# Attention into a gated MLP: 8 block transfers a pair in place of 16, two T buffers, two shared slots for the probabilities, four separate convolution products

## The chip, the cores and the metric

One core of a Trainium2 chip runs the whole program in one launch. The metric is the time of one execution in microseconds. Five queues of instructions run beside each other and wait for one another by semaphores: TensorE (PE, with its weight loads as PEld), VectorE (DVE), ScalarE (ACT), GpSimd (POOL) and SyncE (SP), which here issues nearly all transfers. The sixteen DMA engines that carry out the transfers belong to no queue of instructions.

## The reference

Decay attention over 8 batches of 8 heads, 576 positions, 64 wide, and behind it a gated MLP with a causal convolution of 5 taps:

```python
scores = (q @ k.T) / 8 ; decay = cum[:, None] - cum[None, :]      # cum = cumsum(log(clip(f)))
scores = where(causal, -1e9, scores + decay)
attn = exp(scores - max) ; attn = attn / (sum(attn) + 1e-9)
x = (attn @ v) laid out as (batch, seq, 512)
gate = sigmoid(sum_k conv_w[k] * x[t - 4 + k])                    # 5 taps, per channel
out = (gate * (x @ w_val)) @ w_out
```

## The kernel before, in words

The work is cut into 32 pairs, i = 0 to 31: two heads of one batch. Four pairs make a batch, and the MLP of a batch (`plan_moe`) follows when its four pairs are done.

A pair goes through these steps. `load_pair` brings q and k (`Xr`, two buffers), `load_rest` v (`vt`). `plan_t` splits `Xr` into a rounded part `Xh` (a copy, L286) and a rest `Xl` (a subtraction, L399). `plan_s` makes the scores in four groups u = 0 to 3: the key tile of 576 columns (tile 3), of 448 (tile 2), of 320 and 192 together (tiles 1 and 0), and the last 64 rows. PE writes scores to PSUM; DVE adds the mask and takes the row minimum of the negated scores (L478); ACT takes the exponential into SBUF (L482), for tiles 3 to 0 into `Pt`, which has a place of its own for each tile and head, one set for all pairs, and for the last rows into `Pl`. The sums become reciprocals on DVE (L491, L492), which go by way of DRAM (`zd`) into `zb`, spread over the partitions.

`plan_pt` turns the probabilities. DVE transposes 32 x 32 blocks of each tile from `Pt` into `Tt` (L515, four instructions a pair of 1152, 896, 640 and 384 elements for both heads) and of `Pl` (L518). What is turned inside a block has still to move to other partitions: that is a transfer from `Tt` to `U` (two buffers) for each of 4 groups of 32 partitions and 2 halves of the columns, and each in two pieces m, one with tile 3 (576 columns) and one with the rest (992): 16 transfers of 32 partitions each, issued on SP by the helper `load` (L298). There is one `Tt`, so the transposes of pair i + 1 wait until the transfers of pair i that read the same piece have landed. `plan_pv` multiplies `U` with `vt`, scales by `zb` into `x32` (L563, L286), splits that into `xh` and `xl` (L286, L575), and makes the gate: for pairs 0 to 3 by matmuls with diagonal weights `dg`, for the other 28 by five taps, the first a product (L291 or L293), the next `NA - 1` each a product into `tm` (L291 or L293) and an addition (L606), the rest a fused multiply-add on DVE (L608). Then tanh (L610). `plan_moe` makes value (`Mv`) and output (`Mo`) matmuls, with H (L636), `hh` (L286), `hl` (L650) and the output copy (L677) between.

The two weight matrices are loaded in four pieces each and decoded from 64-bit words (`plan_w`, `decode`), by turns in the memory of `ot` and in `wu`.

What runs when is not left to a scheduler at run time. Every step is a node with the engines it may run on and an estimated duration; the order of all nodes, the engine of each and the PSUM bank of each result are read from the constant `ORDER`, a compressed list of numbers (node times 8 plus an engine code). So each queue runs its steps strictly in the order of the list, and a step that has to wait holds everything behind it on its queue.

## Time and profile before

| | us |
|---|---|
| time, median of 3 runs | 645.98 (645.62 to 647.64) |
| profiled execution, its own time | 645.04 |
| profiled execution, span from the first to the last instruction | 643.3 |

The page gives for each engine its busy time in the span. A busy share is an average over stages: the start (weights, masks, first pairs) and the end (the last MLP) look different from the long middle, in which pair follows pair. A wait is put down to what came last, and an idle stretch of an engine that nobody waits for costs nothing.

### The profile page before, as it was taken

Reading aid. Unit: us, or ns where it says so; the run is one execution under the profiler, and the core shown is the slowest. Engines: PE = TensorE matmul, PEld = TensorE weight load, DVE = VectorE, ACT = ScalarE, POOL = GpSimd, SP = SyncE. Lnnn points to the kernel's source line nnn. Section 1 sums busy time; section 2 is a strip of 40 time slices with the busy share of each in tenths; the row PEclk is TensorE's granted clock in tenths of the full one; section 3 lists DMA queues with packets and bytes.
Section 4 is the critical chain, followed back from the end, with each engine's and each line's share of the span. In section 5 each row is a group of like instructions: output and inputs, shape, how many; then the busy total and the mean of one; then the engine's idle time right before and its main releaser. Section 6 shows DMA issues by size and latency. Waiting matters only on the chain.

```text
span 643.3 us, 16239 instructions
## 1 busy us (share of the span) xinstructions
PE 519.6 (81%) x6096; PEld 451.4 (70%) x6096; DVE 460.6 (72%) x1163; ACT 326.0 (51%) x912; POOL 248.9 (39%) x283
## 2 busy tenths in 40 slices
...
GB/s 236 102 233 196 213 199 165 196 137 121 128 207 223 189 170 178 154 190 165 185 186 207 193 204 188 187 179 197 227 167 210 213 171 191 232 146 154 143 34 82
DMA packets 62558, 114.12 MB, mean 177 GB/s; under 512 B 15760, under 2 KB 32144, under 8 KB 62480
## 3 DMA queue, kind: packets, MB, share of 16 engines
...
q14 instruction: 30, 0.25, 0.1%
...
## 4 chain that ended last, share of the span: by engine, by line
DMA 28%; PE 25%; SPq 20%; DVE 15%; ACT 5%; issue 4%; POOL 1%; DVEq 0%; ACTq 0%; POOLq 0%
PE banks L271 25%; SPq L298 20%; DMA Xr<-in_x_dram 13%; DMA U<-T 7%; DVE banks L478 4%; DVE T L515 4%; DMA zb<-zd 2%; ACT P L482 2%; DMA zd<-zt 2%; DMA vt<-in_v_dram 2%; DVE gate L608 2%; ACT Xh L286 1%; DMA ot<-in_w_val_dram 1%; DVE x L563 1%; DMA gate<-in_f_dram 1%
## 5 line engine op out<-in xcount | busy, mean ns | idle before, releaser
L482 ACT ACTIVATE P<-banks,negm 128x192 f32<-128x192 f32 (+3 forms) x256 | 145.8, 580 | 51.4 <-DVE negm L478 50.6
L515 DVE STREAM_TRANSPOSE T<-P 128x896 f32<-128x896 f32 (+3 forms) x128 | 119.1, 956 | 53.7 <-DMA U<-T 44.7
L478 DVE CUSTOM_DVE_ANT_0 banks<-banks,mk 128x320 f32<-128x320 f32 (+3 forms) x256 | 137.4, 581 | 26.6 <-PE banks L271 17.1
L271 PE MATMUL banks<-U,vt 64*64 64x128 f32 (+1 forms) x3456 | 120.3, 284 | 36.4 <-DMA U<-T 25.9
L271 PEld LDWEIGHTS banks<-U,vt 64*64 64x64 f32 x3456 | 115.0, 152 | 47.3 <-issue 20.7
L271 PE MATMUL banks<-xh,wall 128*128 128x288 f32 x512 | 122.1, 323 | 26.1 <-ACT P L482 16.6
L271 PEld LDWEIGHTS banks<-xh,wall 128*128 128x128 f32 x512 | 93.2, 208 | 32.1 <-ACT P L482 18.9
L271 PE MATMUL banks<-wall,hh 128*128 128x512 f32 x288 | 95.8, 415 | 1.4 <-DVE x L563 1.2
L271 PE MATMUL banks<-st,pkr 64*128 64x288 f32 (+3 forms) x320 | 56.0, 383 | 34.8 <-ACT P L482 10.7
L271 PE MATMUL banks<-xl,wall 128*128 128x288 f32 x256 | 80.9, 316 | 1.8 <-DVE xl L575 1.8
L399 POOL TENSOR_TENSOR Xl<-Xr,Xh 128x512 fp32r<-128x512 f32 (+1 forms) x40 | 56.5, 1425 | 36.8 <-issue 10.2
L271 PEld LDWEIGHTS banks<-st,pkr 64*128 64x128 f32 x320 | 32.6, 205 | 50.4 <-ACT P L482 13.5
L606 POOL TENSOR_TENSOR gate<-gate,tm 128x576 f32<-128x576 f32 x42 | 60.2, 1433 | 13.5 <-DVE gate L606 4.5
L271 PEld LDWEIGHTS banks<-wall,hh 128*128 128x128 f32 x288 | 54.2, 198 | 14.1 <-DVE x L563 1.6
L271 PE MATMUL banks<-wall,hl 128*128 128x512 f32 x144 | 58.3, 405 | 0.4 <-DVE hl L650 0.4
L286 ACT CAST Xh<-Xr 128x512 fp32r<-128x512 f32 (+1 forms) x37 | 22.4, 644 | 68.1 <-DMA Xr<-in_x_dram 68.1
L271 PEld LDWEIGHTS banks<-xl,wall 128*128 128x128 f32 x256 | 53.3, 208 | 2.2 <-DVE xl L575 2.0
L482 ACT ACTIVATION_READ_ACCUMULATOR P<-banks,negm 128x1 f32 x256 | 51.7, 202 | 0.0
L563 DVE TENSOR_TENSOR x<-banks,zb 128x256 f32<-128x256 f32 x64 | 24.4, 415 | 36.2 <-ACT x L286 30.2
L608 DVE SCALAR_TENSOR_TENSOR gate<-x,cw,gate 128x576 f32<-128x576 f32 x56 | 48.8, 883 | 0.8 <-POOL gate L606 0.5
L575 POOL TENSOR_TENSOR xl<-x,xh 128x576 fp32r<-128x576 f32 x25 | 35.6, 1424 | 14.1 <-ACT xh L286 14.1
L500 POOL TENSOR_SCALAR Pl<-Pl,zr 128x64 f32<-128x64 f32 x32 | 15.0, 469 | 66.7 <-DVE zr L491 66.6
...
## 6 DMA issues: line engine op xcount, KB each, us to landing
U<-T SPq DMA_DIRECT2D x256, 124.0 KB, 2.9
Xr<-in_x_dram SPq DMA_DIRECT2D x32, 608.0 KB, 6.3
...
U<-T SPq DMA_DIRECT2D x256, 72.0 KB, 3.2
...
ot<-in_w_val_dram SPq DMA_DIRECT2D x2, 512.0 KB, 5.6
wu<-in_w_val_dram SPq DMA_DIRECT2D x2, 512.0 KB, 6.9
```

The costliest lines, as they stand in the source:

```text
L271: nc.tensor.matmul(out, lhsT=lhsT, rhs=rhs, start=start, stop=stop)
L286: (eng.copy if eng is nc.scalar else eng.tensor_copy)(out=out, in_=in_)
L298: lambda e: (nc.sync if e == "SP" else nc.scalar).dma_start(out=out, in_=in_), reads, writes, **kw)
L399: eng.tensor_tensor(out=Xl[r][:, a - XQ:e - XQ], in0=Xr[r][:, a:e], in1=Xh[r][:, a - XQ:e - XQ].bitcast(F32), op=ALU.subtract)
L478: nc.vector.tensor_tensor_reduce(out=sl, in0=sl, in1=add, op0=ALU.add, op1=ALU.min, scale=-0.125, scalar=3.0e38, accum_out=negm[r][:, col])
L482: nc.scalar.activation(out=dst, in_=bank(key)[:, a0:a0 + ext], func=AF.Exp, bias=negm[r][:, col], scale=-1.0, accum_out=zs[r][:, col])
L500: pool("Pn", 0.25, p + 0.02, lambda: nc.gpsimd.tensor_scalar(out=Pl[r], in0=Pl[r], scalar1=zr[r][:, 8:9], scalar2=0.0, op0=ALU.mult, op1=A ...
L515: dve("DT", dt(2 * w), base + 0.35 + 0.03 * n, lambda t=t, w=w: nc.vector.transpose(out=blocks(FO[t], [(32, 2), (64, 2 * t + 3), (CW, 2)]) ...
L563: nc.vector.tensor_tensor(out=bass.AP(to.tensor, to.offset, [to.ap[0], (P, 4), (32, 2), (1, 32)]), in0=bank(keys[n])[:, 0:L0 // 2].rearran ...
L575: any_("xl", {"POOL": 1.4, "DVE": 0.67}, p, lambda eng: eng.tensor_tensor(out=xl[s], in0=xv, in1=xh[s][:, :].bitcast(F32), op=ALU.subtract ...
L606: any_("cva", {"POOL": 1.4, "DVE": 0.67}, pp, lambda eng, to=to: eng.tensor_tensor(out=gt, in0=gt, in1=to, op=ALU.add), [tk, gk], [gk])
L608: dve("conv", 0.78, pp, lambda src=src, wt_=wt_: nc.vector.scalar_tensor_tensor(out=gt, in0=src, scalar=wt_, in1=gt, op0=ALU.mult, op1=ALU ...
```

## The change

1. The two pieces m of each transfer become one: 8 transfers a pair of 32 partitions x 1568 columns, each waiting for all five transposes of the pair.
2. `Tt` has two buffers, `Ts[i % 2]`. Inside it tile 3 now lies behind tile 2 and the last rows at the end.
3. `Pt` is gone. Tiles 3 and 1 of both heads share `Pa`, tiles 2 and 0 share `Pb`: the exponentials of tile 1 wait for the transpose of tile 3, those of tile 0 for that of tile 2, and those of the next pair's tiles 3 and 2 for those of tiles 1 and 0.
4. `NA` goes from 3 to 5: the two fused multiply-adds become two products and two additions each, so 28 pairs have 56 fused steps fewer and 56 products and 56 additions more.
5. Memory: `dg` lies in `tm`; the second staging place of the value weights lies in `gate` 2 and 3, and the output weights have one staging place, `ot`.
6. The estimates of some steps (`hold` is the time that an issue is thought to take on SP) and with them the whole `ORDER` are new. Decoded, the list has 464 issues on SP in place of 720. Of the additions L606 64 are on POOL and 48 on DVE (before: 42 and 14); of the products into `tm` 101 are on ACT, 10 on POOL and 1 on DVE (42, 10, 4); of the first taps 14 on ACT, 5 on POOL, 9 on DVE (7, 20, 1); of the subtractions L399 all 56 on POOL (40, and 16 on DVE). On PE the list has the same 378 steps. Between the last score step of pair i and the step PV of pair i there lie on average 17.7 other PE steps (pairs 4 to 29), before 17.3. The copies L286 of `Xr` of pairs 11 to 27 (all on ACT) stand behind exponentials of the pair before, i - 1, in all 17 cases; in the list before they stood behind exponentials of pair i - 2 in 12 of the 17. The load of `Xr` of pair i stands in SP's list behind steps of pair i - 3 in nearly all cases, in both lists.

```diff
 L0 = NB * P
 NF = 4
 NCV = 4
-NA = 3
+NA = 5
 NWARM = 6
 NN = 9
 BIG = 8.0e9
...
 BOFF = [sum(EXT[:t]) for t in range(NB)]
 SW = sum(EXT)
 NJ = 9
-FO = [0, 192, 512, 992]
-LO = 960
-CW = 1568
+FB = [0, 3, 8, 15]
+LO = 24 * 2 * 32
+CW = LO + 32
 XZ, XQ, XK, XW = 0, P, P + L0, P + L0 + S
 XP = ((XQ, XK), (XK, XW))
 HW = XW - XQ
 MS = 0.2222
 ORDER = (
 ...
 )
 
 
...
     Xr = tiles(NQ, [P, XW], F32, "Xr")
     Xh = tiles(NQ, [P, HW], F32R, "Xh")
     Xl = tiles(1, [P, HW], F32R, "Xl") * NQ
-    dg = const.tile([P, KC * P], F32, name="dg")
-    tm = tiles(2, [P, S], F32, "tm")
-    Pt = const.tile([P, 2, SW], F32, name="P")
+    tmw = const.tile([P, 2 * S], F32, name="tm")
+    tm = [tmw[:, n * S:n * S + S] for n in range(2)]
+    dg = tmw[:, 0:KC * P]
+    Pa, Pb = (const.tile([P, 2, EXT[t]], F32, name=f"P{t}") for t in (3, 2))
     Pl = tiles(1, [P, D], F32, "Pl") * NQ
-    Tt = const.tile([P, 2 * CW], F32, name="T")
+    Ts = tiles(NQ, [P, 2 * CW], F32, "T")
     U = tiles(NQ, [P, 2, CW], F32, "U")
     vt = tiles(NQ, [P, NJ, 2, D], F32, "vt")
     negm = tiles(NQ, [P, NN], F32, "negm")
...
     ot = [otw[:, n] for n in range(2)]
     wall = const.tile([P, 4, DM // P, DM], F32R, name="wall")
     wvh, wvl, woh, wol = (wall[:, n] for n in range(4))
-    wu = [otw.rearrange("p a d -> p (a d)").bitcast(I32), const.tile([P, 2 * DM], I32, name="wu")]
+    wu = [otw.rearrange("p a d -> p (a d)").bitcast(I32), gall.rearrange("p g s -> p (g s)")[:, 2 * S:2 * S + 2 * DM].bitcast(I32)]
     gflat = gall.rearrange("p g s -> p (g s)")
     wz, wh = gflat[:, 4 * S:4 * S + DM], gflat[:, 5 * S:5 * S + DM]
     wm = wh.bitcast(I32)
...
                 a0 = 224 if u == 0 else c0
                 tr = mk[:, S - ext:] if u < 3 else tri
                 tkey = ("mk",) if u < 3 else ("tri",)
-                dst = Pt[:, h, BOFF[j]:BOFF[j] + ext] if u < 3 else Pl[r]
-                pkey = ("P", h, j) if u < 3 else ("Pl",)
+                dst = (Pa if j % 2 else Pb)[:, h, 0:ext] if u < 3 else Pl[r]
+                pkey = ("P", h, j % 2) if u < 3 else ("Pl",)
                 pp = p + 0.01 * n
 
                 def red(key=keys[n], col=col, a0=a0, ext=ext, add=tr):
...
                                          scale=-1.0, accum_out=zs[r][:, col])
                 dve("red", ext / 960.0 + 0.085, pp, red, [keys[n], tkey], [("red", i, c), ("negm", r, c)])
                 act("SX", ext / 1200.0 + 0.237, pp, ex, [keys[n], ("red", i, c), ("negm", r, c)], [pkey, ("zs", r, c)])
+            plan_pt(i, ((0,), (1,), (2, 3), ())[u])
         p = base + 0.55
         any_("rec", {"DVE": 0.2, "POOL": 0.2}, p, lambda eng: eng.tensor_scalar(
             out=zr[r][:, 0:NN], in0=zs[r], scalar1=1e-9, scalar2=None, op0=ALU.add), [("zs", r, c) for c in range(NN)], [("zr", r)])
...
         for h in range(2):
             src = zq[4 * h:4 * h + 1, :]
             load("zD", 0.4, p + 0.03, zb[r][D * h:D * h + D].rearrange("p (n x) -> p n x", x=P),
-                 bass.AP(src.tensor, src.offset, [(0, D), (32 * 32, 4), (1, P)]), [("zd", i % 4)], [("zb", r, h)], hold=0.45)
+                 bass.AP(src.tensor, src.offset, [(0, D), (32 * 32, 4), (1, P)]), [("zd", i % 4)], [("zb", r, h)], hold=0.68)
         pool("Pn", 0.25, p + 0.02, lambda: nc.gpsimd.tensor_scalar(
             out=Pl[r], in0=Pl[r], scalar1=zr[r][:, 8:9], scalar2=0.0, op0=ALU.mult, op1=ALU.add), [("Pl",), ("zr", r)], [("Pl",)])
 
-    def plan_pt(i):
+    def plan_pt(i, which):
         r = i % NQ
         base = float(i) if i else -6.0
+        Tt = Ts[r]
         pitch = Tt.ap[0]
 
         def blocks(off, dims):
             return bass.AP(Tt.tensor, Tt.offset + off, [pitch, *dims, (1, 32)])
 
         def dt(n):
-            return 0.13 + 0.00113 * n
-        for n, t in enumerate((3, 2, 1, 0)):
+            return 0.045 + 0.001086 * n
+        for n, t in ((0, 3), (1, 2), (2, 1), (3, 0)):
+            if n not in which:
+                continue
             w = EXT[t]
             dve("DT", dt(2 * w), base + 0.35 + 0.03 * n, lambda t=t, w=w: nc.vector.transpose(
-                out=blocks(FO[t], [(32, 2), (64, 2 * t + 3), (CW, 2)]), in_=Pt[:, :, BOFF[t]:BOFF[t] + w]),
-                [("P", 0, t), ("P", 1, t)], [("T", t)])
-        dve("DT", dt(64), base + 0.5, lambda: nc.vector.transpose(out=blocks(LO, [(CW, 2)]), in_=Pl[r]), [("Pl",)], [("T", 4)])
+                out=blocks(64 * FB[t], [(32, 2), (64, 2 * t + 3), (CW, 2)]), in_=(Pa if t % 2 else Pb)[:, :, 0:w]),
+                [("P", 0, t % 2), ("P", 1, t % 2)], [("T", r, t)])
+        if 4 not in which:
+            return
+        dve("DT", dt(64), base + 0.5, lambda: nc.vector.transpose(out=blocks(LO, [(CW, 2)]), in_=Pl[r]), [("Pl",)], [("T", r, 4)])
         for n in range(4):
             for c in range(2):
                 a = D * (n // 2) + 32 * c
-                for m, (o, w, ks) in enumerate(((FO[3], CW - FO[3], (3,)), (0, FO[3], (0, 1, 2, 4)))):
-                    load("U", 0.1 + w / 3100.0, base + 0.45 + 0.1 * m + 0.01 * n, U[r][a:a + 32, n % 2, o:o + w],
-                         Tt[32 * n:32 * n + 32, CW * c + o:CW * c + o + w], [("T", k) for k in ks], [("U", r, n, c, m)], hold=0.4)
+                load("U", 0.6, base + 0.55 + 0.01 * n, U[r][a:a + 32, n % 2], Tt[32 * n:32 * n + 32, CW * c:CW * c + CW],
+                     [("T", r, k) for k in range(5)], [("U", r, n, c)], hold=0.63)
 
     PVJ = []
     for j in range(NJ):
...
                 o = bank(keys[n])
                 for h in range(2) if ts else (n,):
                     hs = slice(D * h, D * h + D)
-                    c = FO[ts[0]] + 32 * h if ts else LO
+                    c = 64 * FB[ts[0]] + 32 * h if ts else LO
                     one = u0[hk, 0, c:c + 32]
-                    gap = [(FO[ts[1]] - FO[ts[0]], 2)] if len(ts) == 2 else []
+                    gap = [(64 * (FB[ts[1]] - FB[ts[0]]), 2)] if len(ts) == 2 else []
                     if ts:
                         one = u0[hk, 0, c + 64 * j:c + 64 * j + 32]
                     src = bass.AP(one.tensor, one.offset, [one.ap[0], *gap, (CW, 2), (1, 32)])
                     dst = o[hs, D * ts[0]:D * ts[-1] + D] if ts else o[hs, L0 // 2:L0 // 2 + D]
                     mm(dst, vt[r][hk, j, h], src, j == 0 and len(ts) == 2 and ts[0] == 0, j == 7 + n)
-        pe("PV", 2.8, base + 0.6, go, [("vt", r), *(("U", r, n, c, m) for n in range(4) for c in range(2) for m in range(2))], keys, cols=12800, mode=4)
+        pe("PV", 2.95, base + 0.6, go, [("vt", r), *(("U", r, n, c) for n in range(4) for c in range(2))], keys, cols=12800, mode=4)
         for n in range(2):
             def ev(n=n):
                 to = xr[:, T0 + D + D * n:T0 + D + D * n + 32]
...
         gt, gk = gate[i % NG], ("gate", i % NG)
         if i < NCV:
             dt = dg
-            dk = [("dg",)]
+            dk = [("tm", 0), ("tm", 1)]
 
             def diag(eng):
                 eng.tensor_tensor(out=dt.rearrange("p (t x) -> p t x", x=P), in0=ident[:, None, :].to_broadcast([P, KC, P]),
...
     def plan_w(nm, src, hi_, lo_, p0):
         for c in range(G):
             hi, lo = hi_[:, c], lo_[:, c]
-            w = c % 2
+            w = c % 2 if nm == "wv" else 0
             p = p0 + 0.7 * c
-            uk = [("ot", 0), ("ot", 1)] if w == 0 else [("wu",)]
+            uk = [("ot", 0), ("ot", 1)] if w == 0 else [("gate", 2), ("gate", 3)]
             kl = [("lw", w)]
             load(nm + "D", 1.8, p - 0.5, wu[w], src[c * P:(c + 1) * P].bitcast(I32), (), uk + kl)
             y = decode(nm, p, wu[w], wm, wz, wh, uk, kl)
...
         load_rest(i)
         plan_t(i)
         plan_s(i)
-        plan_pt(i)
+        plan_pt(i, (4,))
         plan_pv(i)
         if i % G == G - 1:
             plan_moe(i // G)
```

## Rows read from the trace of the kernel before

**Rows 1.** The page's head and its first part: each engine's busy time, share of the span and number of instructions.
```profile
span 643.3 us, 16239 instructions
PE 519.6 (81%) x6096; PEld 451.4 (70%) x6096; DVE 460.6 (72%) x1163; ACT 326.0 (51%) x912; POOL 248.9 (39%) x283
```
**Rows 2.** The windows view, by stage: from and to in us, the length, busy us (and number of instructions) of PE, PEld, DVE, ACT and POOL, then the granted clock of TensorE (1.00 is 2.4 GHz), the share of time that the DMA engines were busy, and GB/s. The first three rows are start, middle and end; the last two are two stretches of the middle.
```profile
0.00:60.00 60.00, 43.54 (x284) 33.13 (x284) 42.70 (x115) 32.59 (x90) 15.33 (x40) 0.77 0.66 198
60.00:605.00 545.00, 442.57 (x5544) 389.02 (x5545) 400.53 (x1011) 285.56 (x810) 233.55 (x243) 0.89 0.69 183
605.00:643.30 38.30, 33.52 (x270) 29.21 (x268) 17.34 (x38) 7.83 (x14) 0.00 (x0) 0.98 0.19 70
460.00:500.00 40.00, 32.11 (x378) 28.74 (x379) 24.64 (x63) 25.96 (x75) 21.87 (x21) 0.83 0.76 197
500.00:540.00 40.00, 37.09 (x460) 33.47 (x461) 32.33 (x85) 24.46 (x72) 21.89 (x26) 1.00 0.72 187
```
**Rows 3.** The windows view of the instructions that read `U` alone (the 108 matmuls of each PV step), in the middle: PE and PEld busy and number, clock, DMA share, GB/s.
```profile
60.00:605.00 545.00, 113.48 (x3240) 108.46 (x3240) 0.89 0.69 183
```
**Rows 4.** The waits view of PE, from 60 to 605 us: what PE waited for, us in total, how often, the longest.
```profile
PE banks L271 <- ACT P L482: 32.3, 19, 5.8
PE banks L271 <- DMA U<-T: 24.8, 9, 5.5
PE banks L271 <- ACT x L286: 13.9, 6, 4.7
PE banks L271 <- DVE x L563: 10.1, 7, 2.4
PE banks L271 <- DVE h L636: 8.5, 6, 3.7
```
**Rows 5.** The waits view of all engines, from 60 to 605 us: three rows of ACT and DVE.
```profile
ACT Xh L286 <- DMA Xr<-in_x_dram: 68.1, 17, 6.1
ACT P L482 <- DVE negm L478: 48.2, 41, 5.8
...
DVE T L515 <- DMA U<-T: 40.6, 17, 5.2
```
**Rows 6.** The page's fourth part, the chain of work that ended last: shares of the span by engine (SPq is SP's queue with its issues).
```profile
DMA 28%; PE 25%; SPq 20%; DVE 15%; ACT 5%; issue 4%; POOL 1%; DVEq 0%; ACTq 0%; POOLq 0%
PE banks L271 25%; SPq L298 20%; DMA Xr<-in_x_dram 13%; DMA U<-T 7%; DVE banks L478 4%; DVE T L515 4%; DMA zb<-zd 2%; ACT P L482 2%; DMA zd<-zt 2%; DMA vt<-in_v_dram 2%; DVE gate L608 2%; ACT Xh L286 1%; DMA ot<-in_w_val_dram 1%; DVE x L563 1%; DMA gate<-in_f_dram 1%
```
**Rows 7.** The timeline of SP in the middle: start, us, and what was issued, like issues one after the other in one row.
```profile
466.21 5.47 SPq L298 DMA_DIRECT2D U<-T  x8
471.78 0.53 SPq L298 DMA_DIRECT2D zd<-zt  x1
472.41 5.51 SPq L298 DMA_DIRECT2D U<-T  x8
477.96 1.30 SPq L298 DMA_DIRECT2D zb<-zd  x2
479.36 0.55 SPq L298 DMA_DIRECT2D vt<-in_v_dram  x1
480.07 0.33 SPq L298 DMA_DIRECT2D Xr<-in_x_dram  x1
```
**Rows 8.** The page's sixth part: transfers, number of issues, KB each, median us from issue to landing.
```profile
U<-T SPq DMA_DIRECT2D x256, 124.0 KB, 2.9
Xr<-in_x_dram SPq DMA_DIRECT2D x32, 608.0 KB, 6.3
...
U<-T SPq DMA_DIRECT2D x256, 72.0 KB, 3.2
...
ot<-in_w_val_dram SPq DMA_DIRECT2D x2, 512.0 KB, 5.6
```
**Rows 9.** The page's fifth part: groups of instructions, all shapes of a line together: busy us, mean ns of one, then the idle time before them.
```profile
L482 ACT ACTIVATE P<-banks,negm 128x192 f32<-128x192 f32 (+3 forms) x256 | 145.8, 580 | 51.4 <-DVE negm L478 50.6
L515 DVE STREAM_TRANSPOSE T<-P 128x896 f32<-128x896 f32 (+3 forms) x128 | 119.1, 956 | 53.7 <-DMA U<-T 44.7
...
L399 POOL TENSOR_TENSOR Xl<-Xr,Xh 128x512 fp32r<-128x512 f32 (+1 forms) x40 | 56.5, 1425 | 36.8 <-issue 10.2
...
L606 POOL TENSOR_TENSOR gate<-gate,tm 128x576 f32<-128x576 f32 x42 | 60.2, 1433 | 13.5 <-DVE gate L606 4.5
L608 DVE SCALAR_TENSOR_TENSOR gate<-x,cw,gate 128x576 f32<-128x576 f32 x56 | 48.8, 883 | 0.8 <-POOL gate L606 0.5
```
**Rows 10.** The groups view with shapes kept apart: the products and additions of the convolution, and the subtraction of `plan_t` on DVE.
```profile
L291 ACT ACTIVATE tm<-x,cw 128x576 f32<-128x576 f32 x42 | 30.6, 770 | 14.5 <-DVE x L563 13.9
L606 DVE TENSOR_TENSOR gate<-gate,tm 128x576 f32<-128x576 f32 x14 | 11.8, 841 | 0.9 <-ACT tm L291 0.4
L399 DVE TENSOR_TENSOR Xl<-Xr,Xh 128x576 fp32r<-128x576 f32 x9 | 8.6, 951 | 0.4 <-ACT Xh L286 0.3
```
**Rows 11.** The timeline, DVE and POOL at two places: an addition of the convolution on DVE with POOL idle (the next POOL instruction starts at 423.20), and one beside a POOL instruction.
```profile
421.13 0.76 DVE L606 TENSOR_TENSOR gate<-gate,tm 128x576 f32<-128x576 f32 x1
...
558.04 1.75 POOL L286 CAST Xh<-Xr 128x512 fp32r<-128x512 f32 x2
558.11 1.15 DVE L606 TENSOR_TENSOR gate<-gate,tm 128x576 f32<-128x576 f32 x1
```

More of the change, by code (lines that the diff above doesn't have):

```diff
@@ new lines @@
+    "KLFFDbi#iIKZ3Qv<H$kyGuRPW7km_c7xn};4z{H9!r#DN!N%d&VGm%=lp**c_&n?bYzf>C_Q0m$w_#Uc3D`9FDLf224x0m$fNii<@EO<!m<a#?3b>A1gs;MP"
+    "0!wfp<s)nzPDr_pLZ(ntI4QxDy#N~!rHB9>pa9H3EX4)Xq?}55j0gay5lDD_3Kb5(3Gj=E?v$;-9O43kgjhzf;R}c{Kn&Nw`w=UM%PCAm6EKX}lQIbmAT|&$"
+    "Q$`SnQ??*G0W*9ir4D%`r4`);OduTawUmP?4am1Cw^B}|%%?yRF`yM_2R2j2Qb0&QJchWJf<^QKlPP;rX~+RUhwKN~NEFhHJeVp%;*kNQ961MkM7fark*&z%"
+    "$X}2TQKLu#x+B$qI)enzJ*gPfxl}6p4bqN6qFIPV6az&@T}z!tNl+h<OQ=Uk4w{deMLk2RQLCuW$S267Xfr~NxQlv)tWEm`m;yS{=aDd!4k18yp+$%XsO!i@"
@@ new lines @@
+    "z=>D}wjf^O6zCvg1-OE&MhDPZ^lhXC{T5e?-T<8FC>jN6M%N-Pp&QY=5dCNXatr+eO@M&$%jkP(Je~pBm3A|=71e|Y5ohsGOmi9^@;tRAZ8(*OaiAtrXV4?5"
+    "N#b(q7<wvoBb9_%Nu5hoVXzo*+8SDl5kgRD^XMq57Bz_upqQA$skpRilo1ocC?E|e3uF^rgE@-QL7b2isWyx#Z9j^ZCQoyvvD0*ENsK>jH_@C{kEu@kiP(XP"
+    "rFk)DQODBI_|CKd<b2vLOb_a}w0;a7e<f`?O@hPVsv$851E<E-L0I^^X=GdrrUTQAX~*z!dmui1H|BcUgESHTCgvby4OfSk<1b-8r^WCM_%~@fd=>t7ngO?o"
+    "Gvgm)Jh*235awChQ;Z7_!?i%}V?LxUV(hqXNEp`+>49`YUZuUpjAQyC?=ZuVLCACbA^a$0jJ%BBz&wJi;3GH}=@=1=og{bT+wnd4etZXh7(amDPkaIy!B60)"
@@ new lines @@
+    "@t^RuxEf*;4vjrYtj0Cs>WNoz_lf<)bGQ~94%<z9Po9NL5C@19><jW7v4<$Y0t60rfrugK2{P<3af)~hM<(d77Q!;ojP;Q`gwIqrHbxpwe@Cn$NeE#AjK(0W"
+    "LKY!+3G0w$h!1;!peFoD7LhiH=Lvj*oJ1o%Ab?3b2`EwodxXFyeIh3ac+wTZcC3zcoUoTrjopR4PN37a5iBH7`WZqUsTnJ#-6phP8%eTsRQfg20n#xnEgheJ"
+    "gyc$Rr|Z&BV*TlZBvJY^k~#e>_A{vu8%uvgdPTa4y-R|Td$9oY4e1H#e)^X5VJwFHfHaYgf{tL%lRl6h5(v<#bS14WolKUHyVD!e+tV53E2N(E=JewvHF=fR"
+    "k<O*Hr1Qx;8U5*JNV9|)@)BX1K!@&SXlRRs!Sofv1a><OOq?grrFY;q2p_SF>Ako&>7Z14Mk{RycZ|_U`;gv7JI4sn9%Gwm7Fv`xi2I!Gq&>xQGDdOZI73D?"
@@ new lines @@
+    "4VLkdmdHR7HRJ{C@eF&$?>K<|2D>ezlZK?zi3c)fac45BnUahTSOU?Lah7%@1DVPpM#)0r&J1;ih3q72iRUu{<Z#9%#xxC+QAHl5?ag4N4$>OP&oZxM^wP#@"
+    "rx+L-IpZo#kV;B@l{rgWqz%z_ke6wF3^GkYl&2a}pE3yaCbEUdOzq2{(e0^DVk?<PZzBikqYQLb7g<VQWQ;RDWezfy7^ldN)B}vsjKPfYjG>Gn#wtTaKf;L7"
+    "Ut~;W_)=~3X~sI^H2o6!D%nWCOyAA~m|pq}{f~?b^rehO<`{iC3&FfWZ(<&%&(jCV4$2<-Bt4o6$s#a^$hYVx=p3euqF_>)HS~jY3)4ptGKpCp_C30jsiA0@"
+    "HL3OV7-c;p#tgIHXILnXtN^o$QlHw&q-51mkd$`jE($<7&HR<A$l6DtQizlb%s`el>nNp_63wd4I!WPDI9at>&*_($-4tQg1oIZNF-u6f!Gva7vU(_M%zI2;"
```

122 lines of the change are left out of this document (48 added, 74 removed).

## The prediction

> **What bounds the kernel now.** I read the page's busy times first [rows 1]: PE has 519.6 of 643.3 us, DVE 460.6, ACT 326, POOL 249. No engine is full, so the span is PE's work and the waits that stand in it. Then the stages [rows 2]. The start takes 60 us and the end 38.3, and the change does nothing in either that could weigh much; what counts is the middle, 545 us, in which PE is busy for 442.6 and idle for 102.4. The matmuls that read `U` number 3240 there [rows 3], 108 to a PV step, so the middle holds 30 pairs: 18.2 us a pair, of them 14.8 busy and 3.4 idle. One stretch of 40 us has PE at 37.1 with the clock at 1.00 (2.4 GHz throughout), its neighbour 32.1 at 0.83 (part of it at 1.2 GHz): the same work goes denser where nothing holds it.
>
> Next, what ends PE's idle time [rows 4]: 32.3 us for ACT's exponentials (a score result can't be written because the bank still holds an older one), 24.8 for `U`, 24.0 for the two copies that empty the PV banks (L286, L563), 8.5 for H. These name the last link only. What ACT and DVE wait for [rows 5] is the link before: ACT stands 68.1 us at the copy of `Xr`, whose load has not landed, and 48.2 at minima from DVE; DVE stands 40.6 us at a transpose into `T`, because the transfers of the pair before still read it. Queues go in order, so while ACT stands at `Xr` the exponentials behind it stand too, and while DVE stands at `T` the next minima do. The chain says the same [rows 6]: 28% transfers, 20% SP's own issues, 25% PE.
>
> Last, SP [rows 7]. Two times eight pieces of `U` take 5.47 and 5.51 us, two `zb` 1.30, `zd` 0.53, `vt` 0.55, `Xr` 0.33: 13.7 us of issues for a pair that lasts 18.2, without the outputs. Eight small pieces (72 KB) cost what eight large ones (124 KB) do [rows 7, 8], some 0.69 us each: the price is per issue, not per byte. And the load of the next `Xr` stands behind all of them.
>
> **Eight transfers, not sixteen.** Eight issues a pair go: 5.5 us of SP's 13.7, leaving 8.2. The bytes stay (196 KB in one, for 124 and 72), so the DMA engines' 69% [rows 2] stays. What is lost is the early half: no piece can start before the last transpose. From then to the last landing it was 8 issues (5.5 us) and some 3 us [rows 7, 8]; it is now the same 8 issues and the landing of a larger piece, between 3 us and, by the nearest load of 512 KB, 5.6 [rows 8]; I take 4, one us more. It is covered: the list leaves 17.7 PE steps between a pair's last scores and its PV step, of 378 for 32 pairs, or 1.5 pairs, about 27 us at the present pace, against 4.6 us of exponentials, 3.8 of transposes [rows 9], 5.5 of issues and 4 of landing, 18 in all. If that cover were gone, each us late would cost 30 us.
>
> A rule speaks against a gain here. The Trainium skill, in "DMA: Bandwidth & Descriptors", section "Issuing engines are not separate DMA queues", says that the time to initiate a transfer is usually small beside the transfer itself. By that rule fewer issues would free next to nothing, and the sum would be the 630 us of the second case below. The trace differs: eight issues take 5.5 us where one piece lands 2.9 us after its issue [rows 7, 8].
>
> **Two `T` buffers.** DVE's 40.6 us at the transposes go nearly whole, since transfers now have a pair's time to read their buffer. DVE's wait is not PE's, so I count only what PE gains. Its 24.8 us for `U` [rows 4] are nine waits in pairs whose pieces came late, because SP was behind and the transposes were held by the pair before. Both causes go. I take 20, between 0 and 24.8. Next to be late is the minimum or the exponential.
>
> **The new list.** It moves the copy of `Xr` on ACT behind exponentials of the pair before, where 12 of 17 stood two pairs back, while its load keeps its place on a shorter SP queue. Half a pair or more of room is more than the mean wait of 68.1 / 17 = 4.0 us and than the longest, 6.1 [rows 5]. So most of the 68.1 goes, and with the 40.6 of DVE the exponentials come earlier; PE's 32.3 us for them [rows 4] then loses between 0 and all. I take half, 16, since the rest is ACT waiting for minima that PE's own lateness causes. PE's 24.0 for the PV copies: between 10 worse (more is queued on ACT) and 15 better; I take 5 better.
>
> **Two more separate taps.** 56 fused steps of 0.883 us leave DVE: 49.4 us. 56 products come, and with the other moves ACT has 59 more: 59 x 0.770 = 45 us. Of 56 more additions 34 are on DVE, 34 x 0.841 = 29 us, and 22 on POOL, 22 x 1.433 = 32 us [rows 9, 10]. 16 subtractions go from DVE to POOL: about 15 us off DVE, 16 x 1.425 = 23 us on POOL [rows 9, 10]. So DVE falls by some 35 us to 425, ACT rises to about 371 and POOL to about 304. None passes PE, and DVE's relief is already in the 16 above, so I count it at nothing. The cover is idle ACT and POOL; without it the gate, H and the value banks behind it come late, at most by the 1.4 and 1.7 us a pair by which ACT and POOL are longer.
>
> An addition on DVE takes 0.76 us with POOL idle and 1.15 beside a POOL instruction [rows 11]; were all 34 beside POOL, that adds 34 x 0.39 = 13 us to DVE and not to the path. The Trainium skill, in "SBUF — State Buffer", section "SBUF: two separate sides", holds that the pair of ports which the two share is locked for a whole instruction and the loser blocks fully. By that rule each of the 34 could lose a full POOL addition, 1.43 us, or 49 us of DVE time, which would eat the relief. The trace shows 0.39 in this case.
>
> **Shared slots and memory.** The exponentials of tiles 1 and 0 now wait for DVE. Bounds: nothing, if transposes are done in time, and the price of the third case. I take 3 us. The output weights, loaded one after the other, can hold SP or the first output by between 0 and 5.6 us [rows 8], as they are spread over some four pairs in the list; I take 1.
>
> **Sum.** 645.04 - 20 - 16 - 5 + 3 + 1 = 608 for the profiled execution, whose span is 643.3. The median is 0.9 us above it, so 609. Of PE's 102.4 us idle in the middle some 65 stay.
>
> **The rivals.**
> Second case, SP's time was covered: what SP issues fast still waits for transposes and for PE to free `Xr`, and ACT goes on standing there. Then only the second `T` gives: half of the 24.8 and a quarter of the 32.3, 20 us, less 4: 629, 630 at the median. For it: SP was idle for part of each pair. Against it: `Xr` lands 6.3 us after its issue [rows 8], and SP issues 13.7 us of 18.2.
>
> Third case, slower: the shared slots turn DVE and ACT into one loop. Eight exponentials a pair take 8 x 0.580 = 4.6 us and four transposes 4 x 0.956 = 3.8 [rows 9]. Exponentials of tile 1 wait for the transpose of 3, the next pair's for that of 1, and each queue is in order. If nothing else on DVE ran beside the exponentials, a pair would take 8.4 us and DVE's other work, (425 - 119) / 32 = 9.6: 18.0 us, against 18.2 now. From 0.2 us of handing over or of other ACT work inside the loop it decides; at 0.7 us, 18.7 x 30 + 98.3 = 659. Against it: minima and convolution steps can run beside exponentials, which makes the loop far shorter than the pair.
>
> Fourth case, no change: what SP and DVE give is taken back by the longer ACT and POOL lists at the gate. Their 3.1 us a pair would be 93 us at most; 37 of them cancel the gain, which leaves about 646.
>
> **How the numbers follow.** 0.58 for the first case, with a range of its own from 588 to 622: at the low end the waits for `U` and for exponentials go whole (57 us), at the high end about 23 us go in all. 0.24 for the second, 622 to 643. 0.05 for the fourth and 0.13 for the third. The range 587 to 643 leaves out the third and fourth and a little of the first: 2 in 10 at most. A measurement of this kernel can tell about 0.3%, 2 us, from no change. Faster 0.82, same 0.05, slower 0.13.
>
> **What would show it.** Right: DVE's wait at L515 for `U` near nothing; ACT's wait for `Xr` under 25 us; SP with 464 issues; PE's wait for `U` under 5 us and its busy share at 85% or more; DVE near 425 us. Wrong in the second way: ACT still some 50 us at `Xr`. In the third: ACT at L482 waiting for L515, or DVE at L515 for L482, by tens of us. In the fourth: PE waiting for H or for x. If PE waits for `U` as before, the lost early half was worth more than the one us above.

## The result and the profile after

The kernel after takes 571.84 us (median of 4 runs, 569.91 to 575.21), the kernel before 645.8 beside it: a ratio of 0.8855, 95% interval 0.8804 to 0.8906. The forecast was 609 us with a range from 587 to 643: the sign was right, the size half of what came, and the time lies below the range. The profiled execution took 569.91 us. Medians are of all runs; the ratios leave out runs that took over 1.5% longer than the fastest run of the same kernel.

The page of after, its head and its first part, answering to [rows 1]:

```profile
span 568.2 us, 15877 instructions
PE 486.0 (86%) x6096; PEld 419.9 (74%) x6096; DVE 445.7 (78%) x1150; ACT 369.9 (65%) x968; POOL 293.0 (52%) x296
```

The same 6096 products took 519.6 us before and take 486.0 now. PE's idle time is span less busy time: 123.7 us before, 82.2 now. So the 75.1 us by which the span fell are 41.5 of idle time and 33.6 of busy time. The windows view of after by stage (columns as in [rows 2]) shows where:

```profile
0.00:60.00 60.00, 40.82 (x377) 30.81 (x377) 46.86 (x127) 29.76 (x80) 16.90 (x44) 0.74 0.74 211
60.00:534.00 474.00, 415.25 (x5545) 363.17 (x5547) 386.41 (x993) 331.32 (x875) 273.91 (x251) 0.96 0.80 210
534.00:568.20 34.20, 29.97 (x185) 25.95 (x176) 12.40 (x30) 8.87 (x15) 2.19 (x2) 1.00 0.14 55
```

The middle holds as many products as in [rows 2], to one, and is 71 us shorter: 43.7 us less idle (102.4 to 58.7) and 27.3 less busy (442.6 to 415.3). Beside that stands the clock, 0.89 before and 0.96 now. What PE still waits for there (waits view of PE, 60 to 534 us, answering to [rows 4]):

```profile
PE banks L262 <- DMA U<-T: 14.9, 8, 5.0
PE banks L262 <- ACT P L473: 11.6, 12, 1.8
PE banks L262 <- DVE h L632: 10.2, 9, 3.8
PE banks L262 <- DVE x L559: 8.0, 8, 2.4
...
PE banks L262 <- ACT x L277: 1.2, 1, 1.2
```

Exponentials fell from 32.3 to 11.6, `U` from 24.8 to 14.9, the two PV copies from 24.0 to 9.2, and H rose from 8.5 to 10.2. The link before, the waits view of ACT and DVE in the same stretch, answering to [rows 5]:

```profile
ACT Xh L277 <- DMA Xr<-in_x_dram: 27.5, 14, 4.5
ACT P L473 <- DVE negm L469: 26.3, 36, 3.1
DVE T L510 <- ACT P L473: 14.2, 23, 2.5
```

DVE's 40.6 us for `U` at the transposes are down to 1.8. The chain of work (the page's fourth part) has SP's queue at 8% where [rows 6] has 20%:

```profile
DMA 27%; PE 25%; DVE 19%; ACT 10%; SPq 8%; issue 6%; POOL 5%; DVEq 0%; POOLq 0%; ACTq 0%
```

And the transfers (the page's sixth part, as [rows 8]): a whole block lands 4.8 us after its issue, where a piece took 2.9 or 3.2.

```profile
U<-T SPq DMA_DIRECT2D x256, 196.0 KB, 4.8
Xr<-in_x_dram SPq DMA_DIRECT2D x32, 608.0 KB, 6.8
```

Why does the same product take less time? Groups of PE by shape, first in the two neighbouring stretches of before in [rows 2], at a clock of 0.83 (460 to 500 us) and of 1.00 (500 to 540 us), then in a stretch of after at 1.00 (340 to 380 us); the number after the comma is the mean ns of one:

```profile
L271 PE MATMUL banks<-xh,wall 128*128 128x288 f32 x32 | 11.3, 444 | 6.0 <-ACT P L482 6.0
L271 PE MATMUL banks<-xl,wall 128*128 128x288 f32 x16 | 6.9, 433 | 0.0
```
```profile
L271 PE MATMUL banks<-xh,wall 128*128 128x288 f32 x48 | 10.3, 301 | 1.9 <-DVE x L563 1.2 <-ACT P L482 0.7
L271 PE MATMUL banks<-xl,wall 128*128 128x288 f32 x24 | 7.1, 294 | 0.0
```
```profile
L262 PE MATMUL banks<-xh,wall 128*128 128x288 f32 x32 | 6.9, 301 | 0.0
L262 PE MATMUL banks<-xl,wall 128*128 128x288 f32 x16 | 4.7, 294 | 0.0
```

At 2.4 GHz they last the same in both kernels, 301 and 294 ns; in the stretch with 0.83 they last 444 and 433. The kernel after is not doing cheaper products, it does more of them at the upper of the two clocks. The traces know two levels of the clock, 0.50 and 1.00, so a mean clock c over a span S means S x 2 x (1 - c) at 1.2 GHz: 144 us before (0.888), 65 after (0.943). Not all of that is busy time. The windows view of the stretches at 0.50 alone ends with their sum, first of before, then of after (us, then the busy us of each engine in them):

```profile
sum 144.54, PE 116.19 PEld 104.60 DVE 103.84 ACT 78.96 POOL 50.99; mean PE 5.28 PEld 4.75 DVE 4.72 ACT 3.59 POOL 2.32
```
```profile
sum 64.85, PE 46.16 PEld 38.66 DVE 46.66 ACT 29.74 POOL 17.99; mean PE 4.62 PEld 3.87 DVE 4.67 ACT 2.97 POOL 1.80
```

So PE works 116 us at 1.2 GHz before and 46 after. What PE did before the clock fell stands in the windows view of before, from 460 to 470 us; the last three columns are clock, DMA share and GB/s:

```profile
460.00:462.00 2.00, 0.00 (x0) 0.00 (x0) 0.00 (x0) 1.68 (x4) 0.00 (x0) 0.81 1.07 296
462.00:464.00 2.00, 1.24 (x5) 1.24 (x6) 0.00 (x0) 2.00 (x8) 1.84 (x2) 0.50 0.95 228
464.00:466.00 2.00, 2.00 (x10) 2.00 (x9) 1.20 (x1) 2.00 (x9) 2.00 (x2) 0.50 0.71 176
466.00:468.00 2.00, 2.00 (x11) 2.00 (x10) 1.51 (x5) 1.26 (x5) 0.91 (x3) 0.50 0.65 163
468.00:470.00 2.00, 2.00 (x28) 1.68 (x31) 1.60 (x3) 0.00 (x0) 1.22 (x2) 0.98 0.96 298
```

PE had stood 5.06 us for an exponential. When it starts again it is fully busy, at a clock of 0.50 (1.2 GHz), until 468 us. This gap is paid twice: while it lasts, and in the products behind it.

### The profile page after: what moved, and what is told of

Same layout as the page of the kernel before. It is cut to its first block, busy times and chain, and to the rows that moved or that the text cites. A ratio compares the mean times of both kernels' runs of the same rounds, so it can differ in the third digit from the quotient of the medians.

```text
span 568.2 us, 15877 instructions
## 1 busy us (share of the span) xinstructions
PE 486.0 (86%) x6096; PEld 419.9 (74%) x6096; DVE 445.7 (78%) x1150; ACT 369.9 (65%) x968; POOL 293.0 (52%) x296
## 4 chain that ended last, share of the span: by engine, by line
DMA 27%; PE 25%; DVE 19%; ACT 10%; SPq 8%; issue 6%; POOL 5%; DVEq 0%; POOLq 0%; ACTq 0%
PE banks L262 25%; DMA Xr<-in_x_dram 13%; SPq L289 8%; DMA U<-T 8%; DVE T L510 6%; DVE banks L469 5%; ACT P L473 4%; DMA out_dram<-ot 2%; POOL Xl L390 2%; DMA zb<-zd 1%; ACT Xh L277 1%; DVE x L559 1%; DVE gate L602 1%; DMA cwu<-in_conv_w_dram 1%; ACT tm L282 1%
## 5 line engine op out<-in xcount | busy, mean ns | idle before, releaser
L469 DVE CUSTOM_DVE_ANT_0 banks<-banks,mk 128x192 f32<-128x192 f32 (+3 forms) x256 | 137.8, 579 | 14.8 <-PE banks L262 9.3
L510 DVE STREAM_TRANSPOSE T<-P 128x640 f32<-128x640 f32 (+3 forms) x128 | 120.3, 962 | 21.6 <-ACT P L473 14.9
L262 PE MATMUL banks<-U,vt 64*64 64x128 f32 (+1 forms) x3456 | 112.2, 271 | 28.6 <-DMA U<-T 18.9
L262 PEld LDWEIGHTS banks<-U,vt 64*64 64x64 f32 x3456 | 106.6, 143 | 38.0 <-issue 20.8
L262 PE MATMUL banks<-xh,wall 128*128 128x288 f32 x512 | 113.5, 305 | 7.5 <-ACT P L473 4.5
L602 POOL TENSOR_TENSOR gate<-gate,tm 128x576 f32<-128x576 f32 x64 | 90.9, 1421 | 33.9 <-DVE gate L602 11.3
L390 POOL TENSOR_TENSOR Xl<-Xr,Xh 128x512 fp32r<-128x512 f32 (+1 forms) x56 | 78.3, 1415 | 47.0 <-PE banks L262 20.9
L262 PEld LDWEIGHTS banks<-xh,wall 128*128 128x128 f32 x512 | 85.6, 191 | 14.2 <-ACT P L473 5.9
L282 ACT ACTIVATE tm<-x,cw 128x576 f32<-128x576 f32 x101 | 76.5, 775 | 17.9 <-DVE gate L602 12.1
L571 POOL TENSOR_TENSOR xl<-x,xh 128x576 fp32r<-128x576 f32 x28 | 40.5, 1446 | 32.3 <-ACT xh L277 19.2
L602 DVE TENSOR_TENSOR gate<-gate,tm 128x576 f32<-128x576 f32 x48 | 40.7, 848 | 8.3 <-ACT tm L282 7.5
L277 ACT CAST Xh<-Xr 128x512 fp32r<-128x512 f32 (+1 forms) x38 | 23.5, 644 | 32.5 <-DMA Xr<-in_x_dram 32.4
```

The source lines that it names most:

```text
L262: nc.tensor.matmul(out, lhsT=lhsT, rhs=rhs, start=start, stop=stop)
L277: (eng.copy if eng is nc.scalar else eng.tensor_copy)(out=out, in_=in_)
L282: eng.activation(out=out, in_=in_, func=AF.Copy, scale=col)
L390: eng.tensor_tensor(out=Xl[r][:, a - XQ:e - XQ], in0=Xr[r][:, a:e], in1=Xh[r][:, a - XQ:e - XQ].bitcast(F32), op=ALU.subtract)
L469: nc.vector.tensor_tensor_reduce(out=sl, in0=sl, in1=add, op0=ALU.add, op1=ALU.min, scale=-0.125, scalar=3.0e38, accum_out=negm[r][:, col])
L510: dve("DT", dt(2 * w), base + 0.35 + 0.03 * n, lambda t=t, w=w: nc.vector.transpose(out=blocks(64 * FB[t], [(32, 2), (64, 2 * t + 3), (CW, ...
```

## Experiments

All ratios are to the kernel before, run beside each. Differences in us are to the median of after, 571.84, or of before in the same call (644.2 to 646.6); after itself was not run again beside them. Waits are those of the whole span, where PE's for `U` are 25.9 us before and 18.9 after, and those for exponentials 39.6 and 23.3.

### Undoing one part

**Sixteen issues again (e1).** Each block of `U` leaves as two pieces, at the same place in SP's list:

```
-  load("U", ..., U[r][a:a + 32, n % 2], Tt[..., CW * c:CW * c + CW], ...)
+  for lo, hi in ((0, 992), (992, CW)):
+      nc.sync.dma_start(out=U[r][a:a + 32, n % 2, lo:hi], in_=Tt[..., CW * c + lo:CW * c + hi])
```

> The changed kernel, but each of its 8 transfers a pair is issued as two pieces (992 and 536 or 576 columns) one behind the other at the same place of SP's list; two T buffers, slots, taps and list stay. Theory A (what gained was the sum of shorter issues on SP, the second T and the new list, each a part, and TensorE's clock adds to each): 256 issues of some 0.6 us come back on SP, U lands about 5 us later in each pair, PE idles 15 to 30 us more, its matmuls take 5 to 20 us longer at a lower clock: 592 to 620 us. Rival B (the new list alone gained, SP's issue time is covered): 568 to 578 us.

Measured: 658.37 us, ratio 1.0157 (1.008 to 1.0233), 87 us over after. The whole gain and more is gone, beyond what either theory allowed. PE's wait for `U` is 36.8 us, ACT's for `Xr` 77.5 (32.4 after), PE is busy 521.9 us at a clock of 0.887.

**One `T` (e2).** All pairs share one buffer; 64 of DVE's 804 steps had to move, so that the list stays possible:

```
-    Ts = tiles(NQ, [P, 2 * CW], F32, "T")
+    Ts = tiles(1, [P, 2 * CW], F32, "T") * NQ
```

> The changed kernel with one T for all pairs in place of two; where the list had a transpose of the next pair ahead of a transfer that still reads T, the DVE steps are put behind it (64 of 804 move), nothing else moves. Theory A: DVE stands 20 to 50 us at L510 for U again, PE idles 15 to 40 us more, and the clock falls: 590 to 630 us. Rival B: under 580 us, DVE's wait is hidden.

Measured: 808.13 us, ratio 1.2508 (1.2446 to 1.257), far above both theories. Three rows of its waits view, all engines, show the loop:

```profile
ACT P L471 <- DVE negm L467: 265.8, 70, 13.9
...
PE banks L260 <- ACT P L471: 122.7, 23, 12.6
...
DVE T L508 <- DMA U<-T: 113.9, 16, 9.5
```

DVE stands at a transpose until `U` has left, the minima queued behind it come late, and ACT and PE wait for them. The new list lives on the second buffer. How much of the loss is that of the 64 moved steps was not taken apart.

**Fused taps (e3).** `NA = 3` again, the rest as after.

> The changed kernel with the last two taps fused on DVE again (56 fused steps at the places of the additions; the 56 products and 56 additions go); everything else stays. Theory A: DVE gains some 20 us of work, ACT and POOL lose 43 and 32; none is the bound, so 566 to 580 us. Rival (the relief of DVE was a main source): 585 us and more, with DVE's busy time above 460.

Measured: 573.35 us, ratio 0.885 (0.8784 to 0.8916), as after and as theory A had it. DVE is 30 us busier (475.6) and ACT 35 less (335.2); PE does not notice.

### Doing one part alone

**Copies of `Xr` later (e4).** In before, the 12 early pairs of copies move to the place on ACT where the new list has them; nothing else changes.

> The kernel before, with one thing of the new list: the copies of Xr of the 12 pairs that stood on ACT behind exponentials of pair i-2 now stand behind the third exponential of pair i-1; no other queue's list changes. Theory A: ACT's wait for Xr falls from 68 us to under 35, the exponentials come earlier, PE idles 8 to 20 us less, and with the clock the time is 620 to 636 us. Rival (ACT's wait for Xr was harmless, or S then waits for Xl): 643 us or more.

Measured: 645.15 us, ratio 0.9994 (0.9955 to 1.0033). ACT's wait for `Xr` fell from 68.1 to 25.0 us and its wait for minima rose from 50.6 to 62.6. So 12 of the 43 us turn up at the next wait in the queue. PE gained next to nothing: its idle time is 121.4 us (123.7 before), its wait for `U` 17.9 in place of 25.9 and that for H 16.8 in place of 8.5.

**Eight issues alone (e7).** Before with one transfer a block, one `T`, its own list (10 DVE steps moved):

```
-  for m, (o, w, ks) in enumerate(((FO[3], CW - FO[3], (3,)), (0, FO[3], (0, 1, 2, 4)))):
-      load("U", ..., U[r][..., o:o + w], Tt[..., CW * c + o:CW * c + o + w], [("T", k) for k in ks], ...)
+  load("U", ..., U[r][a:a + 32, n % 2], Tt[..., CW * c:CW * c + CW], [("T", k) for k in range(5)], ...)
```

> The kernel before, with the two pieces of each transfer issued as one at the place of the later piece in SP's list; one T, its own slots, its own list (10 of 826 DVE steps move behind transfers that they must follow). Theory P: 256 issues fewer on SP give most of the gain by themselves, 580 to 610 us. Theory L: the last piece starts no earlier than before, and DVE now stands longer at the one T, so little or nothing is gained, 630 to 670 us.

Measured: 676.94 us, ratio 1.0488 (1.0415 to 1.056), worse than either theory had it. DVE waits 49.4 us for `U` at the transposes (44.7 before), ACT 86.2 for minima (50.6). The reading is that with one `T` losing the early half is worth more than the issues saved; that, and what the 10 moved steps cost, was not taken apart.

### Is it SP's time, and is it per issue?

**Idle issues between those of `U` (e5), or ahead of `zd` (e6).** Eight transfers a pair of 4 bytes a partition, which nobody waits for:

```
+  nc.sync.dma_start(out=dmy[32 * n:32 * n + 32, c:c + 1], in_=ident[32 * n:32 * n + 32, c:c + 1])
```

> The changed kernel with 8 more transfers a pair that nobody waits for: behind each of the 8 issues of U, on SP, one of 32 partitions x 4 bytes between two places of its own. Bytes, U's pieces and all else stay. Theory A2 (what cost the 16-issue kernel its 80 us is SP's time per issue, some 0.6 us each, wherever the bytes are): 256 issues bring it back, 630 to 660 us. Rival D (the cost lay in the pieces themselves: more and shorter packets on the DMA engines): 570 to 590 us.

> The same 8 idle transfers a pair, all ahead of the issue of zd, where SP waits for the reciprocals for 54 us in all. Theory P (SP's queue is full and its sum of issues is the pace): the same time as with the dummies among the U issues, within 10 us. Theory L (SP is not full; what counts is that U lands later behind the last transpose, and the loop from transposes by U, PV and the next scores back to transposes gets longer): part of the dummies lies in SP's idle time, so at least 20 us less than with the dummies among U, 590 to 630 us.

Measured: e5 659.87 us (ratio 1.0245, 1.0172 to 1.0318), e6 643.54 (0.9974, 0.9937 to 1.001). So 256 issues that move next to nothing cost 88 and 72 us; the 16 us between the two come from the place. SP's timeline of e5 (start, us, what was issued):

```profile
330.78 0.59 SPq L522 DMA_DIRECT2D dmy<-ident  x1
331.41 0.59 SPq L521 DMA_DIRECT2D U<-T  x1
332.05 0.59 SPq L522 DMA_DIRECT2D dmy<-ident  x1
```

An issue of 4 bytes a partition holds the queue as long as one of 196 KB: both have a median of 0.59 us over the run. The DMA engines are not what got slower, since in e5 a block of `U` lands 2.8 us after its issue, sooner than the 4.8 of after. The time of e6 lies between what the two theories gave it. The first rule weighed in the prediction (the Trainium skill, "DMA: Bandwidth & Descriptors", "Issuing engines are not separate DMA queues") has the time to initiate usually small beside the transfer. For one block that holds here: 0.59 us of issue, 4.8 to landing. What the prediction drew from it, that fewer issues would free next to nothing, does not hold: on one queue 256 of them make 72 to 88 us.

**More issues off SP (e8, e11, e12).** In after, the 36 outputs leave from ACT (e8), the outputs and 29 loads of `Xr` (e11), and 28 loads of `vt` too (e12).

> The changed kernel with its 36 output transfers issued on ACT, each right behind the copy that fills its buffer, in place of SP, where SP stood 42 us waiting for those copies. Theory P: 36 issues of some 0.4 us less on SP, 14 us of pace: 555 to 563 us. Theory L: what counts is that U, zb and Xr no longer stand behind an output on SP: 560 to 570 us, with SP's wait for the output copy gone; ACT pays 15 us that is covered. Rival: ACT is on the path by now, 575 us or more.

> The kernel after, with the 36 output transfers and 29 loads of Xr issued by ScalarE instead of SyncE, each right behind ScalarE's own step that the transfer waits for. If SyncE's issue time (0.59 us an issue) still sets when U's transfers go out, 38 us less of it lowers TensorE's waits for U (18.9) to 8 to 13 and the time to 550 to 565. If that is over at 8 transfers a pair (the outputs alone on ScalarE gave 568.8 with 17.0 us of waits for U), the time stays at 566 to 576, or rises to 576 to 590 where the issues on ScalarE (65 x 0.4 to 0.6 us) stand in front of its exponentials.

> As the one before, and 28 loads of vt issued by ScalarE too (93 issues in all, some 55 us of SyncE's issue time). SyncE's issues decide still: 545 to 562, waits for U under 10. They no longer decide: 566 to 576. ScalarE's side decides: 576 to 600, with more of TensorE's waits on the exponentials (23.3 after).

Measured: e8 568.78 us (0.8738, 0.866 to 0.8816), with runs from 561.62 to 578.85, so that some us of gain over after are neither shown nor ruled out; e11 588.35, with runs from 578.75 to 590.62, as the last of its cases had it; e12 607.59 (0.9369, 0.9287 to 0.9451), above all that was expected. PE's wait for `U` hardly moves with the issues taken off SP: 18.9 us after, 17.0 in e8, 21.2 in e11, 16.2 in e12. Its wait for exponentials is 31.4 in e12. So what is left of the wait for `U` does not hang on SP's other issues. That ACT's queue is what loses in e11 and e12 is what the waits suggest; it was not taken apart.

### Do gaps set the clock?

**Pauses and filler at the same places (e9, e10).** In after, ahead of each of the 36 output products of the MLP, TensorE's queue gets 24 drains (e9) or three idle products into the bank that the real one then starts afresh (e10):

```
   o = bank(key)
+  if half == 0:
+      for _ in range(24): nc.tensor.drain()                              # e9
+      for jj in range(3): mm(o, wall[:, 0, 0, 0:P], wall[:, 0, 0], True, True)   # e10
```

> The kernel after, with 24 drain instructions in TensorE's queue ahead of each of the 36 output products of the MLP: nothing else is added, no data are touched, so TensorE stands still there for some time (its idle time shows how long; guessed 1 us each, 36 us in all). Theory G (TensorE's granted clock follows its gaps, so time lost in gaps is lost a second time in the products themselves): in the kernel before there was 41 us more idle time than after and 34 us more busy time for the same 6096 products, so here every microsecond of added idle time brings 0.5 to 1 us of busy time; with 36 us added the profile shows a clock of 0.90 to 0.92 (0.943 after), 505 to 520 us busy (486 after), and the time rises by 50 to 75 us, to 620 to 650. Rival F (the busy time fell from before to after for a reason of the changed work, other accesses beside it for example, not through the gaps): the busy time stays 483 to 490, and the time rises by at most the idle time added, to 572 to 608.

> The kernel after, with three further 128x512 products ahead of each of the same 36 output products (108 in all, into the bank that the output product then starts afresh, so the outputs are unchanged): at 0.41 us each they hold TensorE up for 44 us in all at the same places as the pauses of the other kernel, but busy. Theory G: no gap is added, so the 6096 products of the kernel take no longer than after (486 us), the clock stays at 0.94 or above, and the time rises by 15 to 44 us, to 587 to 616: less for each us of delay than with pauses. Rival F: pauses and products of the same length cost the same.

Measured: e9 635.22 us (0.983, 0.9778 to 0.9881), 63.4 over after; e10 579.33 (0.8952, 0.8882 to 0.9022), 7.5 over. The lengths were not equal, so each is taken by its own. A pause lasts 1.72 us (62 us more idle time ahead of the group below than after has there, by 36), and three idle products some 0.7 us (some 26 us in all, by the timeline). Pauses thus cost 1.0 us for each us, filler 0.3. The products behind the pauses, groups by shape, e9 and then after:

```profile
L262 PE MATMUL banks<-wall,hh 128*128 128x512 f32 x288 | 110.1, 468 | 64.3 <-issue 26.7 <-DVE negm L469 10.8 <-ACT tm L282 5.5
```
```profile
L262 PE MATMUL banks<-wall,hh 128*128 128x512 f32 x288 | 93.2, 405 | 2.4 <-ACT x L277 1.2 <-DVE x L559 0.9 <-ACT Pl L473 0.4
```

In e10 the same group takes 396 ns. In e9 PE is busy 506.6 us for the same 6096 products, 20.6 more than after, at a clock of 0.918. One pause close up, windows view of e9:

```profile
305.00:308.00 3.00, 3.00 (x110) 2.93 (x102) 2.63 (x5) 2.79 (x9) 0.00 (x0) 1.00 0.61 153
...
309.20:311.00 1.80, 0.11 (x1) 0.00 (x0) 1.80 (x6) 0.61 (x3) 1.80 (x2) 1.00 1.03 245
311.00:311.80 0.80, 0.78 (x3) 0.67 (x4) 0.77 (x5) 0.51 (x3) 0.55 (x1) 0.97 0.94 206
311.80:314.80 3.00, 3.00 (x8) 2.31 (x7) 1.72 (x4) 2.38 (x10) 1.11 (x2) 0.50 0.98 203
...
317.00:320.00 3.00, 3.00 (x30) 2.84 (x27) 3.00 (x9) 2.54 (x7) 2.85 (x3) 1.00 0.82 293
```

PE stands until 311.0, does its first products at 0.97, and then spends 3.0 us fully busy at 0.50. Not every pause does this: by the trace's record of the clock, 15 of the 36 have a fall to 0.50 in them or within 1.4 us behind them, and 21 have none. The price of the lower level, from the timelines of PE: two products with `hl` that follow each other, first in e9 behind that pause, then in e10 (start, us, instruction):

```profile
312.70 0.63 PE L262 MATMUL banks<-wall,hl 128*128 128x512 f32 x1
313.13 1.05 PE L262 MATMUL banks<-wall,hh 128*128 128x512 f32 x2
313.99 0.63 PE L262 MATMUL banks<-wall,hl 128*128 128x512 f32 x1
```
```profile
278.88 0.39 PE L262 MATMUL banks<-wall,hl 128*128 128x512 f32 x1
279.11 0.62 PE L262 MATMUL banks<-wall,hh 128*128 128x512 f32 x2
279.57 0.40 PE L262 MATMUL banks<-wall,hl 128*128 128x512 f32 x1
```

The same three products take 1.29 us from start to start at 1.2 GHz and 0.69 at 2.4, so a busy us at the lower level loses 0.60 / 1.29 = 0.47. e9 came within all that theory G gave it (20.6 us busy, 0.918, 635). e10 came in under its range, with a clock of 0.932 in the profiled run where 0.94 was expected. In e9 the span is 62 us longer: 20.6 in the slower products and 41.4 in idle time, since part of the pauses falls where PE would have waited anyway.

The price accounts for PE's busy time in every kernel here. Take 0.47 of the part at 0.50 off it: 519.6 - 0.47 x 116.2 = 465.0 before, 486.0 - 0.47 x 46.2 = 464.3 after, 506.6 - 0.47 x 87.4 = 465.5 in e9. In the other ten runs with the same 6096 products, their stretches at 0.50 counted in the same way, whose busy times go from 490.1 to 531.0 us, 459 to 468 are left. So rival F, by which the busy time has nothing to do with the gaps, falls, and no other cause of slower products has to be looked for. How much low clock a given gap brings is not settled: e9 has the idle time of before (123.6 and 123.7 us), but 87 us of busy time at 0.50, not 116.

**Filler where PE waits for `U` (e13 in before, e14 in after, e15 on top of e8).** Two idle products ahead of each pair's PV step:

```
+  for m in range(2):
+      mm(bank(keys[0]), st[:, 0:P], st[:, 0:512], True, True)
```

> The kernel before, unchanged but for two further 128x512 products ahead of each pair's product with U (64 in all, from constants into the bank that the pair's first product then starts afresh, so the outputs are unchanged): 26 us of work at 0.41 us each, put where TensorE waits for U (24.8 us in 9 waits). If filled gaps alone buy back clock in this kernel: some 7 us of idle time goes, the 6096 products take 505 to 515 us (519.6 before), and the time is 632 to 648, although 26 us of work came on. If the clock needs the change itself (gaps elsewhere stay): the products take 517 to 521 and the time is 648 to 672.

> The same two products ahead of each pair's product with U in the kernel after, where TensorE waits 18.9 us for U in 9 waits. If the gaps left there cost more than they last: 560 to 572, with a clock over 0.943 and the 6096 products at 475 to 484 us. If not, the 26 us of added work cost what the 44 us of the filled output products did, 0.17 us for each (7 us of 44): 573 to 580.

> The same two products on top of the outputs issued by ScalarE (568.8 by itself): 555 to 570 where filled gaps pay, 570 to 578 where they cost 0.17 us for each.

Measured: e13 644.0 us (0.9991, 0.9963 to 1.0019): added work for nothing, with the clock at 0.899 (0.888 before), but also no gain: PE still works 113.2 us at 0.50, against 116.2. e14 566.49 us (0.879, 0.8736 to 0.8845), clock 0.960, idle 66.6 us (82.2 after), 36.3 us of work at 0.50 (46.2); e15 570.33, no faster than e8. In after, too, the work is free; whether e14 is faster than after stays open, since their intervals overlap.

## Why the prediction was wrong, step by step

**The step that failed is the sum.** "645.04 - 20 - 16 - 5 + 3 + 1" has terms for PE's idle time only, and carries PE's busy time over as it was. The idle time was nearly right: 65 us were to stay in the middle, 58.7 did. The busy time was not constant: 33.6 us of it went. The prediction had the row for this: of the two stretches of [rows 2] it named the clock and that "the same work goes denser where nothing holds it", but the sum got no term for it. At the 0.47 us that a busy us at 1.2 GHz loses (e9, e10), the 70 us less of such work (116.2 to 46.2) are 33 us, against 33.6 measured. Had the sum let the 116 us shrink with the gaps, by the 37 of 102 that it took off, it would have had 42 x 0.47 = 20 us more, 589 in place of 609. That is an estimate, and it still misses by 17: the work at 1.2 GHz fell by 60%, PE's idle time in the middle by 43%.

That the idle time came out nearly right is in part luck, as none of its terms did: 9.9 came for the 20 of `U`, 20.7 for 16, 14.8 for 5, and H lost 1.7. Of the signs that the prediction named, DVE's wait at the transposes (1.8 us), the 464 issues and PE's 86% came; ACT's wait for `Xr` stayed at 27.5 us for under 25, PE's for `U` at 14.9 for under 5, and DVE's busy time at 445.7 for 425.

**Eight transfers, not sixteen.** Counted at nothing by itself and one us later landing; it decides, together with the second `T`. Issues given back cost 72 to 88 us (e1, e5, e6). But the issues saved in before cost 31 us (e7), which also lost the early half and kept the single `T`. That a lost early half is covered fits after, with two buffers, and does not fit e7, with one.

**Two `T` buffers.** The 40.6 us of DVE went, as said. PE's wait for `U` fell by 9.9 us, not 20: SP's eight issues take 5.86, 6.56 and 8.46 us in three pairs of its timeline, and a block lands 4.8 us after its issue. The second cause, the pair before, was gone; the first was only halved.

**The new list.** The reason given for its 16, the copies of `Xr` behind other exponentials, is worth nothing alone (e4). The second `T` was not tried with the old list, so what the new list adds to eight issues and two buffers stays open. The runs do show that the parts hang together: the list needs two buffers (e2), list and buffers together need the fewer issues (e1), and the fewer issues alone lose (e7).

**Two more separate taps.** Nothing, as forecast (e3). DVE ended at 445.7 us, not 425: 16 more copies of `pl` stand on it (15.8 us where it had 5.1) and 8 more first products (7.5 us where it had 0.5). The second rule weighed, the full lock of the shared ports (the Trainium skill, "SBUF — State Buffer", "SBUF: two separate sides"), does show, and the prediction read it wrong. Ten of the 48 additions on DVE began when a POOL instruction had run for 0.1 us or more and had as much left; each ended some 0.6 us after that instruction, so that they took from 0.76 to 1.79 us. One of them in the timeline of after (start, us, instruction):

```profile
415.74 1.40 POOL L571 TENSOR_TENSOR xl<-x,xh 128x576 fp32r<-128x576 f32 x1
...
416.36 1.39 DVE L602 TENSOR_TENSOR gate<-gate,tm 128x576 f32<-128x576 f32 x1
```

POOL ends at 417.14, the addition at 417.75. The 0.39 us that the prediction took from [rows 11] was thus no fixed price: it hangs on how much of the POOL instruction was left. The lock cost little because meetings are rare. Against the 0.76 us of an addition alone these ten lost some 5 us in all, and the mean of the 48 is 848 ns, 841 before.

**Shared slots and memory.** The 3 and 1 us can't be told in a result of this size. ACT waits 0.3 us at an exponential for a transpose, so the third case has no row.

**The rivals.** The second, SP's time covered, falls with e5 for the kernel after. The third and the fourth have no rows behind them.
